# Writing the result of attention plus soft mixture of experts as whole rows instead of half rows

## The chip, the cores and the metric

The kernel runs on one core of one Trainium2 chip. The metric is the device time of one execution in microseconds (us). The kernel before takes 460.35 us (median of three runs, 460.24 to 461.63).

## The reference

```python
attn = softmax(0.125 * q @ k.T, causal) @ v          # 8 batches, 12 heads, 448 tokens, head size 64
x = attn, heads side by side                         # 3584 tokens x 768
logits = x @ phi                                     # 3584 x 32 slots
slot_in = softmax(logits, over tokens).T @ x         # 32 x 768, four slots for each of 8 experts
slot_out[e] = relu(slot_in[e] @ w1[e]) @ w2[e]       # w1 768x1024, w2 1024x768
out = softmax(logits, over slots) @ slot_out         # 3584 x 768, float32
```

All of it is float32. The two weight arrays hold 50.3 MB, the result 11.01 MB.

## The kernel before, in words

The first part, some 355 us long, is attention: 96 heads, one after another, with the order of the work on each engine written out by hand (the tuple ORDER). Of its engines only the clock and the queues matter here. While it runs, SyncE (SP) already loads the first 22 weight tiles.

The second part is the experts. Weight tiles of 128 partitions x 1536 floats (768 KB, one contiguous run of 6 KB in each partition) come through SP's queue into 34 buffers. `expert_in(e)` multiplies the slots by w1, `expert_out(e, hf)` by one half of w2's columns, where hf is 0 for columns 0 to 383 of the result and 1 for columns 384 to 767. The loads are ordered so that all tiles for hf = 0 come first, and the 16 tiles for hf = 1 last.

When `expert_out` has gone through all experts with hf = 0, `slots(0)` brings their sum into the form that the last matmul needs. It is a chain over three engines: VectorE copies the sum `so` out of PSUM, TensorE spreads it with a matmul into `rp`, ScalarE copies `rp` rounded into `sr`, and VectorE subtracts to leave the rounding rest in partitions 64 to 127 of `sr`. Then `combine(t, 0, ...)` runs for fourteen tiles t of 256 tokens, two after each `expert_out(e, 1)`. Each makes two matmuls of 128 tokens (u = 0 and 1, tile `pp`); ScalarE takes the first out of PSUM and VectorE the second, into `ot`; then SP issues one DMA of 384 KB that writes 256 pieces of 1536 bytes, half a row of the result each. After the last `expert_out` come `slots(1)` and fourteen `combine(t, 1, ...)` in the same way. So 28 DMAs write the result, and all of them stand in SP's queue behind all the weight loads. Eight DMAs of this queue are in flight at most: each has a completion semaphore out of a set that is reused in turn, and SP waits until the one it takes is free.

Every engine runs its instructions in the order in which the program issues them (`_InOrder`). `warm(n, w)` puts n matmuls on TensorE whose results nobody reads.

Of the kernel before, what the change touches and what calls it, by code (L numbers as in the profile page):

```python
# [9 lines left out]
F32 = mybir.dt.float32  # L10
F32R = mybir.dt.float32r
BF16 = mybir.dt.bfloat16
AF = mybir.ActivationFunctionType
ALU = mybir.AluOpType
# [3 lines left out]
P = 128  # L18
# [4 lines left out]
NT = NB * S  # L23
# [8 lines left out]
NR, XB = 2, 3  # L32
RES, TW1 = 22, 12
WN, PAD = 1536, 24
WARM = (3, 3, 6, 3)
START = (6, 7, 4)

# [40 lines left out]
def attention_soft_moe(ctx: ExitStack, tc: tile.TileContext, qk, va, phi, w1, w2, out):  # L80
    nc = _Core(tc)
# [28 lines left out]
    st = {}  # L110
# [11 lines left out]
    def loads_v(p, eng=nc.sync):  # L122
        if p < NPAIR:
# [4 lines left out]
    order = ([(m, e, h, u) for e in range(NEXP) for m, hs in ((0, (0, 1)), (1, (0,))) for h in hs for u in range(2)]  # L128
             + [(1, e, 1, u) for e in range(NEXP) for u in range(2)])
    NBUF = RES + TW1  # L130

    def slot(n, name, dtype=F32):
        m = n % NBUF
        pool, tag = (wres, "w") if m < RES else (wt[0], f"wa{m}")
        return pool.tile([P, WN], dtype, tag=tag, name=name)
# [40 lines left out]
    def misc(name):  # L176
        return ps_1.tile([P, 512], F32, tag="m", name=name)

    def warm(n, w=None):

        w = misc("warm") if w is None else w
        for _ in range(n):
            nc.tensor.matmul(w, identb, tri.unsqueeze(1).to_broadcast([P, w.shape[1] // P, P]),
                             start=True, stop=True)
# [53 lines left out]
    def scores1_all(i):  # L238
        for part in ("c0", "k3", "c3", "c12", "k2", "k1", "k0"):
            scores1(i, part)  # L240

    def max_evac(i):
        if i < NHD:
            st["mx", i] = (xtp.tile([P, 512], F32, tag="xt", name="mx1", bufs=2)[:, 0:S] if i == 1
                           else mx_)
            nc.scalar.activation(out=st["mx", i], in_=st["s", i][:, SC0:SC0 + S], func=AF.Copy)
# [97 lines left out]
    def logits_a(b, js, g, first=True, last=True):  # L344

        for j in js:
            xt = st.pop(("xt", b * PPB + j))
            for c in range(NCH):
                nc.tensor.matmul(g[32 * c:32 * c + 32], phis[j // 3][:, j % 3], xt[:, P * c:P * c + P],
                                 start=first and j == js[0], stop=last and j == js[-1], skip_group_check=True)  # L350
# [5 lines left out]
    def logits_b(b, l):  # L356
        bm = st["bm", b] = moe.tile([P, 1], F32, tag="bm", name=f"bm{b}", bufs=2)
        nc.vector.tensor_reduce(out=bm, in_=l, axis=AX.X, op=ALU.max, negate=True)

        mo, mn = run_m[(b + 1) % 2], run_m[b % 2]  # L360
        nc.vector.tensor_tensor(out=mn, in0=mo, in1=st.pop(("bm", b)), op=ALU.min)
# [46 lines left out]
    for b in range(NB):  # L408
        o, last = 12 * b, b == NB - 1
# [11 lines left out]

    warm(START[0])
    h0, h1 = slice(0, 1), slice(1, 2)
# [6 lines left out]
    scores1_all(1)  # L430
    warm(START[1])
    max_evac(0)
# [11 lines left out]
    scores1_all(2)  # L444
    warm(START[2])
    max_evac(2)
# [9 lines left out]
    srep = const.tile([P, 4, NSLOT], F32, name="srep")  # L456
# [23 lines left out]
    for i in range(NHD + 1):  # L480
        p, h = divmod(i, 2)
# [60 lines left out]
    b = NB - 1  # L542
# [4 lines left out]
    nc.tensor.matmul(lp, ident, lt, start=True, stop=False, skip_group_check=True)  # L547
    warm(WARM[0], wm)
    x = st.pop(("x", NPAIR - 1))
# [5 lines left out]
    logits_a(b, (4,), lp, first=False, last=False)  # L555
    warm(WARM[1], wm)
    for c in range(NCH):
        nc.tensor.matmul(lp[32 * c:32 * c + 32], phis[1][:, 2], xa[:, P * c:P * c + P],
                         start=False, stop=True, skip_group_check=True)
    logits_b(b, lp)  # L560
    warm(WARM[2], wm)

# [8 lines left out]
    for c in range(NCH):  # L571
        nc.tensor.matmul(tm[32 * c:32 * c + 32, P:P + 1], nm[:, 0:NSLOT], ident[:, 0:1],
                         start=True, stop=True, skip_group_check=True)
    warm(WARM[3], wm)
    wc, rz, sidw = (const.tile([P, n], F32, name=m) for m, n in (("wc", 1), ("rz", 1), ("sidw", NSLOT)))
# [10 lines left out]
    for hf in range(2):  # L586
        tps = (po0 if hf == 0 else po).rearrange("p a b->p (a b)")[:, 0:3 * NSLOT]
        for c in range(3):
            o = 384 * hf + P * c
            nc.tensor.matmul(tps[:, NSLOT * c:NSLOT * c + NSLOT], si[:, o:o + P], sidw,  # L590
                             start=True, stop=True)
# [23 lines left out]
    pt2 = pst.enter_context(tc.tile_pool(name="pt2", bufs=2, space=PSUM, reuse_waits="tile"))  # L615
    pso = pst.enter_context(tc.tile_pool(name="pso", bufs=4, space=PSUM, reuse_waits="tile"))
# [57 lines left out]
    so = [pt1.tile([P, 384], F32, name=f"so{i}") for i in range(2)]  # L674
    sr = const.tile([P, DM], F32R, tag="si", name="sr")
# [5 lines left out]
    def expert_out(e, hf):  # L681
        for u in range(2):
            w = wtiles[1, e, hf, u].rearrange("p (f n)->p f n", n=384)
            for g in range(4):
                fc = 4 * u + g
                nc.tensor.matmul(so[hf][32 * g:32 * g + 32], hts[e][:, fc], w[:, g],
                                 start=e == 0 and u == 0, stop=e == NEXP - 1 and u == 1,
                                 skip_group_check=True)

    def slots(hf):  # L690
        sl = slice(384 * hf, 384 * hf + 384)

        sos = c4s[-1][:, 1024:1408].bitcast(F32)
        nc.vector.tensor_copy(out=sos, in_=so[hf])
        rp = pt2.tile([P, 512], F32, tag="h", name=f"rp{hf}")
        nc.tensor.matmul(rp[:, 0:384], srep.rearrange("p a b->p (a b)"), sos, start=True, stop=True)
        nc.scalar.activation(out=sr[:, sl], in_=rp[:, 0:384], func=AF.Copy)
        nc.vector.tensor_tensor(out=sr[64:P, sl], in0=rp[64:P, 0:384], in1=sr[64:P, sl], op=ALU.subtract)

    ov = out.rearrange("(t u p) (a n) -> t p u a n", u=2, p=P, a=2)  # L700
    ntile = NT // (2 * P)

    def combine(t, hf, nb):

        if t % 2 == 0:
            st["ot"] = slot(nb, f"ot{t}_{hf}").rearrange("p (u n) -> p u n", n=384)
        ot = st["ot"][:, 2 * (t % 2):2 * (t % 2) + 2]
        for u in range(2):
            pp = pso.tile([P, 512], F32, tag="o", name=f"pp{t}_{u}_{hf}")
            o = P * (2 * t + u)  # L710
            nc.tensor.matmul(pp[:, 0:384], ct[o // WN][:, o % WN:o % WN + P],
                             sr[:, 384 * hf:384 * hf + 384], start=True, stop=True)
            if u == 0:
                nc.scalar.activation(out=ot[:, u], in_=pp[:, 0:384], func=AF.Copy)
            else:
                nc.vector.tensor_copy(out=ot[:, u], in_=pp[:, 0:384])
        nc.sync.dma_start(out=ov[t, :, :, hf], in_=ot)

    ct, c4s = [], []
    n = NBUF  # L720

    def loads(k):
        nonlocal n
        for _ in range(k):
            load_w(n)
            n += 1
# [19 lines left out]
                combine_t(b)  # L746
    expert_out(NEXP - 1, 0)
    loads(2)
    slots(0)
    for e in range(NEXP):  # L750
        expert_out(e, 1)
        for t in range(2 * e, min(ntile, 2 * e + 2)):
            combine(t, 0, len(order) + 7 + t // 2)
    slots(1)
    for t in range(ntile):
        combine(t, 1, len(order) + 7 + ntile // 2 + t // 2)
    pst.close()


# [41 lines left out]
```

## Time and the profile before

| | us |
|---|---|
| median of three runs | 460.35 |
| time of the profiled execution | 459.88 |
| its span, first to last instruction | 458.2 |
| last weight tile landed | 429.31 |
| `slots(1)` starts, first matmul of `combine(0, 1)` | 430.27, 433.25 |
| last instruction of a compute engine ends | 443.7 |

Times in the profile count from the span's start. PE is TensorE's matmuls, PEld its weight loads, DVE VectorE, ACT ScalarE, SPq the sequencer of SyncE, which issues the DMAs. A row of the windows view holds the stretch, its length, the busy time of PE, PEld, DVE, ACT and POOL with their counts of instructions, then the granted TensorE clock as a share of full speed, the busy share of the sixteen DMA engines (over 1 where packets overlap) and the rate in GB/s. In a timeline row stand start, length, engine and instruction. In a row of DMA issues stand the size of one and the median us from issue to landing.

### The profile page before, as it was taken

To read this page: it belongs to the slowest core of one execution; us is meant where nothing else is said; L and a number is where in the kernel's file an instruction comes from. 1 tells how busy PE (TensorE), PEld (TensorE's weight loads), DVE (VectorE), ACT (ScalarE), POOL (GpSimd) and SP (SyncE) were. 2 spreads that over 40 slices of the span, in tenths; PEclk is the share of its full clock that TensorE was granted. 3 is DMA by queue.
4 is the path that set the end of the run, shared out by engine and by line. 5 is a ranking of instruction groups with operands and counts; after the bars stand their busy time and mean duration, and the time that the engine had idled before them with its cause. 6 is when DMAs were issued, how large, how long until landed. Compare 5 with 4: busy or idle time off the path is not lost.

```text
span 458.2 us, 12014 instructions
## 1 busy us (share of the span) xinstructions
PE 424.9 (93%) x4581; PEld 362.3 (79%) x4581; DVE 348.9 (76%) x1044; ACT 329.9 (72%) x496; POOL 266.3 (58%) x215
## 2 busy tenths in 40 slices
PE   6899999999999999999999999999999998996660
PEld 3798999999899989998999999999989654542230
DVE  6988888888888898888888888888886467332350
ACT  6898899889888988897899789988975211342240
POOL 5888777777777777777778777777771000000000
PEclk9999999999999999999999999999999999999875
DMA  7477666676667765777666766667758999999997
GB/s 267 128 259 243 235 193 224 216 239 223 204 208 237 236 221 171 241 241 231 210 188 225 254 222 216 191 213 253 231 160 300 369 411 415 414 414 413 402 391 284
DMA packets 38201, 119.04 MB, mean 260 GB/s; under 512 B 4096, under 2 KB 11776, under 8 KB 38144
## 3 DMA queue, kind: packets, MB, share of 16 engines
q1 hardware_dynamic: 38000, 118.01, 75.6%
q8 instruction: 36, 0.59, 0.5%
q10 hardware_dynamic: 144, 0.27, 0.2%
q14 instruction: 21, 0.17, 0.1%
HBM read 107.25 MB, written 11.01 MB: 258 GB/s over the span
## 4 chain that ended last, share of the span: by engine, by line
PE 77%; DMA 11%; POOL 5%; ACT 1%; DVE 1%; issue 1%; SPq 0%; POOLq 0%; ACTq 0%
PE po L64 34%; PE s L64 24%; DMA w<-in_w_dram 10%; PE xt L64 4%; PE g L64 3%; PE hp L64 3%; POOL r L64 3%; PE sp L64 2%; PE rt L64 2%; PE pp L64 2%; POOL ks L64 1%; PE e L64 1%; PE so L64 1%; DMA qk<-in_qk_dram 1%; ACT ot L64 0%
## 5 line engine op out<-in xcount | busy, mean ns | idle before, releaser
L64 PE MATMUL po<-va,pt 128*128 128x65 f32 x1900 | 193.6, 250 | 0.1
L64 PEld LDWEIGHTS po<-va,pt 128*128 128x128 f32 x1900 | 190.5, 171 | 0.5 <-issue 0.3
L64 DVE TENSOR_TENSOR mx<-s,mx 128x320 f32<-128x320 f32 (+2 forms) x288 | 100.8, 350 | 31.4 <-ACT mx L64 27.9
L64 POOL TENSOR_TENSOR r<-qk,qd 64x896 fp32r<-64x896 f32 (+1 forms) x50 | 101.5, 2030 | 6.5 <-ACT qd L64 2.7
L64 POOL TENSOR_SCALAR_AFFINE_SELECT r<-mr 14x448 fp32r<-14x448 f32 x96 | 61.4, 640 | 73.2 <-DVE mr L64 72.8
L64 ACT ACTIVATE pt<-s 128x1024 f32<-128x1024 f32 x96 | 98.2, 1023 | 6.3 <-PE s L64 3.1
L64 POOL TENSOR_TENSOR ks<-qk,ks 64x896 fp32r<-64x896 f32 (+1 forms) x47 | 98.1, 2087 | 4.5 <-ACT ks L64 0.9
L64 PE MATMUL s<-r,k 128*128 128x320 f32 (+3 forms) x384 | 83.2, 298 | 2.3 <-POOL r L64 2.2
L64 ACT ACTIVATE mx<-s 128x448 f32<-128x448 f32 x96 | 52.5, 546 | 36.0 <-PE s L64 22.2
L64 PE MATMUL s<-qd,ks 128*128 128x448 f32 (+3 forms) x384 | 76.0, 308 | 1.6 <-ACT qd L64 1.6
L64 PEld LDWEIGHTS s<-r,k 128*128 128x128 f32 (+1 forms) x384 | 60.0, 176 | 6.4 <-POOL r L64 2.9
L64 DVE STREAM_TRANSPOSE mt<-mx 128x448 f32<-128x448 f32 x96 | 61.9, 645 | 3.3
L64 DVE TENSOR_REDUCE r<-mt 128x14 f32<-128x448 f32 x96 | 58.4, 609 | 0.1
L64 PEld LDWEIGHTS s<-qd,ks 128*128 128x128 f32 (+1 forms) x384 | 55.0, 180 | 3.1 <-ACT qd L64 2.3
L64 ACT ACTIVATE ks<-qk 128x896 fp32r<-128x896 f32 (+1 forms) x50 | 45.6, 914 | 2.5 <-DMA qk<-in_qk_dram 2.5
L64 ACT ACTIVATE k<-ks 64x896 fp32r<-64x896 f32 (+1 forms) x49 | 45.8, 935 | 1.1
L64 ACT ACTIVATE qd<-qk 128x896 fp32r<-128x896 f32 (+1 forms) x50 | 46.1, 923 | 0.4 <-DMA qk<-in_qk_dram 0.3
L64 PEld LDWEIGHTS <-identb 128*128 128x128 bf16 x320 | 28.1, 99 | 20.1 <-issue 15.8
L64 DVE TENSOR_TENSOR x<-po,sm 128x256 f32<-128x256 f32 x95 | 40.3, 424 | 3.3
L64 PE MATMUL s<-tri,identb 128*128 128x64 bf16 (+2 forms) x288 | 39.7, 234 | 0.2
L64 ACT ACTIVATE xts<-xt 128x512 f32<-128x512 f32 x47 | 28.1, 598 | 6.7 <-PE xt L64 4.4
L64 PE MATMUL so<-w,ht 128*32 128x384 f32 x256 | 24.9, 492 | 7.4 <-DMA w<-in_w_dram 5.6
(124 smaller groups left out, 396.2 us busy)
## 6 DMA issues: line engine op xcount, KB each, us to landing
w<-in_w_dram SPq DMA_DIRECT2D x64, 768.0 KB, 7.5
qk<-in_qk_dram SPq DMA_DIRECT2D x94, 448.0 KB, 3.5
va<-in_va_dram SPq DMA_DIRECT2D x47, 260.0 KB, 3.5
out_dram<-ot SPq DMA_DIRECT2D x28, 384.0 KB, 6.5
qk<-in_qk_dram SPq DMA_DIRECT2D x4, 224.0 KB, 3.3
va<-in_va_dram ACTq DMA_DIRECT2D x1, 260.0 KB, 5.4
phi<-in_phi_dram SPq DMA_DIRECT2D x2, 48.0 KB, 3.9
```

Source lines behind the costliest of these rows:

```text
L64: return self._tc.keep_in_program_order(op(*args, **kwargs))
```

## The change

1. The DRAM rows are dealt out otherwise: partition p of tile t holds tokens 256t + 2p and 256t + 2p + 1, which lie next to each other in DRAM. The matmul takes every second column of `ct` for it.
2. `ot` of a tile is one buffer for both halves of the columns (two tokens x 768 floats in a partition). For tiles 6 to 13 the first half is only kept, and after the second half one DMA writes the tile: 768 KB, 128 pieces of 6144 bytes. Tiles 0 to 5 (FILL = 6) are written as before, in two DMAs of 384 KB. There are 20 DMAs instead of 28.
3. With hf = 1, tiles 6 to 13 are combined first and tiles 0 to 5 last.
4. `slots(1)` runs its chain twice, for 192 columns each; four idle matmuls stand ahead of the first `rp`, and four behind the second.

```diff
-WARM = (3, 3, 6, 3)
+WARM = (3, 3, 6, 3, 4, 4)
+FILL = 6
...
-    def slots(hf):
...
+    def slots(hf, parts):
+        for a, z in parts:
+            sl = slice(384 * hf + a, 384 * hf + z)
+
+            sos = c4s[-1][:, 1024 + a:1024 + z].bitcast(F32)
+            nc.vector.tensor_copy(out=sos, in_=so[hf][:, a:z])
+            if hf and a == 0:
+                warm(WARM[4], pso.tile([P, 512], F32, tag="o", name="warm1")[:, 0:384])
+            rp = pt2.tile([P, 512], F32, tag="h", name=f"rp{hf}_{a}")[:, 0:z - a]
+            nc.tensor.matmul(rp, srep.rearrange("p a b->p (a b)"), sos, start=True, stop=True)
+            nc.scalar.activation(out=sr[:, sl], in_=rp, func=AF.Copy)
+            nc.vector.tensor_tensor(out=sr[64:P, sl], in0=rp[64:P], in1=sr[64:P, sl], op=ALU.subtract)
+        if hf:
+            warm(WARM[5], pso.tile([P, 512], F32, tag="o", name="warm2")[:, 0:384])
+
-    ov = out.rearrange("(t u p) (a n) -> t p u a n", u=2, p=P, a=2)
+    ov = out.rearrange("(t p u) n -> t p u n", u=2, p=P)
...
+    def combine(t, hf):
+        if hf == 0:
+
+            ots[t] = slot(len(order) + 7 + t, f"ot{t}").rearrange("p (u n) -> p u n", u=2)
+        ot, sl, o = ots[t], slice(384 * hf, 384 * hf + 384), 2 * P * t
         for u in range(2):
             pp = pso.tile([P, 512], F32, tag="o", name=f"pp{t}_{u}_{hf}")
-            o = P * (2 * t + u)
-            nc.tensor.matmul(pp[:, 0:384], ct[o // WN][:, o % WN:o % WN + P],
-                             sr[:, 384 * hf:384 * hf + 384], start=True, stop=True)
+            nc.tensor.matmul(pp[:, 0:384], ct[o // WN][:, o % WN + u:o % WN + 2 * P:2],
+                             sr[:, sl], start=True, stop=True)
...
-        nc.sync.dma_start(out=ov[t, :, :, hf], in_=ot)
+        if t < FILL:
+            nc.sync.dma_start(out=ov[t, :, :, sl], in_=ot[:, :, sl])
+        elif hf:
+            nc.sync.dma_start(out=ov[t], in_=ot)
...
-    slots(0)
+    slots(0, ((0, 384),))
...
-    slots(1)
-    for t in range(ntile):
-        combine(t, 1, len(order) + 7 + ntile // 2 + t // 2)
+    slots(1, ((0, 192), (192, 384)))
+    for t in [*range(FILL, ntile), *range(FILL)]:
+        combine(t, 1)
```

## Rows read from the trace of the kernel before

**Rows 1.** The page, the span in 40 slices: rate of the DMA engines.

```profile
GB/s 267 128 259 243 235 193 224 216 239 223 204 208 237 236 221 171 241 241 231 210 188 225 254 222 216 191 213 253 231 160 300 369 411 415 414 414 413 402 391 284
```

**Rows 2.** Windows view: weight stream, output stream and its parts, and the clock's fall.

```profile
400.00:424.00 24.00, 19.32 (x158) 8.50 (x162) 6.99 (x14) 7.64 (x18) 0.00 (x0) 1.00 1.02 414
...
428.00:457.00 29.00, 11.30 (x43) 6.23 (x38) 8.63 (x17) 6.92 (x15) 0.00 (x0) 0.68 0.99 366
430.00:440.00 10.00, 7.89 (x25) 4.70 (x21) 5.48 (x11) 4.64 (x10) 0.00 (x0) 0.66 1.06 399
444.00:456.00 12.00, 0.00 (x0) 0.00 (x0) 0.00 (x0) 0.00 (x0) 0.00 (x0) 0.54 0.96 352
456.00:457.00 1.00, 0.00 (x0) 0.00 (x0) 0.00 (x0) 0.00 (x0) 0.00 (x0) 0.50 0.13 46
...
430.00:432.00 2.00, 1.32 (x6) 0.30 (x2) 0.56 (x1) 0.00 (x0) 0.00 (x0) 0.85 1.06 399
```

**Rows 3.** Chain that ended last, from the last weight load to `combine(0, 1)`.

```profile
413.94 15.37 DMA w<-in_w_dram
...
430.27 0.57 DVE c L64
...
430.89 1.20 PE rp L64 x2
...
432.63 0.57 DVE sr L64
...
433.25 5.13 PE pp L64 x13
```

**Rows 4.** Timeline of SyncE's queue: loads and writes, one issue a row.

```profile
370.67 0.39 SPq L64 DMA_DIRECT2D w<-in_w_dram  x1
371.21 0.34 SPq L64 DMA_DIRECT2D w<-in_w_dram  x1
...
415.84 0.41 SPq L64 DMA_DIRECT2D out_dram<-ot  x1
...
442.52 1.14 SPq L64 DMA_DIRECT2D out_dram<-ot  x1
443.75 1.13 SPq L64 DMA_DIRECT2D out_dram<-ot  x1
```

**Rows 5.** DMA issues of 400 to 415, 428 to 440 and 451 to 458 us.

```profile
w<-in_w_dram SPq DMA_DIRECT2D x8, 768.0 KB, 15.4
...
out_dram<-ot SPq DMA_DIRECT2D x10, 384.0 KB, 7.5
...
out_dram<-ot SPq DMA_DIRECT2D x3, 384.0 KB, 4.1
```

**Rows 6.** Timeline: `slots(0)`, `combine(8, 0)` at full clock, `combine(0, 1)` at half.

```profile
403.99 0.91 PE L64 MATMUL rp<-c,srep 128*128 128x384 f32 x2 [0.68 <-DVE c L64]
...
418.49 0.97 PE L64 MATMUL pp<-sr,ct 128*128 128x384 f32 x4
...
419.14 1.02 DVE L64 COPY ot<-pp 128x384 f32<-128x384 f32 x2 [2.76 <-PE pp L64]
...
434.29 1.90 DVE L64 COPY ot<-pp 128x384 f32<-128x384 f32 x3 [1.10 <-DMA out_dram<-ot]
```

**Rows 7.** Groups by form, 350 to 445 us, and timeline of `warm`: smaller pieces.

```profile
L64 DVE COPY xta<-e 128x256 f32<-128x256 f32 x1 | 0.4, 425 | 0.8 <-PE e L64 0.8
...
L64 ACT ACTIVATE ct<-cp 128x192 fp32r<-128x192 f32 x1 | 0.3, 328 | 0.0
...
360.50 0.83 PE L64 MATMUL po<-tri,identb 128*128 128x256 bf16 x6
...
362.16 0.50 PE L64 MATMUL po<-tri,identb 128*128 128x256 bf16 x3
```

**Rows 8.** Span's start: SyncE's first issue, and DMA rate in slices of 0.1 us.

```profile
0.81 2.77 SPq L64 DMA_DIRECT2D qk<-in_qk_dram  x6
...
GB/s 0 0 0 0 0 0 0 0 0 0 0 0 0 0 0 0 0 0 90 54 90 143 125 251 340 340 412 412 287 287 358 430 394 394 269 161 143 125 125 90
```

More of the change, by code (lines that the diff above doesn't have):

```diff
@@ L688, in expert_out @@
                                  skip_group_check=True)
-    def slots(hf):
[L691 to L698, printed above, removed]
@@ L700, in attention_soft_moe @@
-    ov = out.rearrange("(t u p) (a n) -> t p u a n", u=2, p=P, a=2)
[L701 to L707, printed above, removed]
+    def slots(hf, parts):
[11 more added lines that the diff above has]
+            warm(WARM[5], pso.tile([P, 512], F32, tag="o", name="warm2")[:, 0:384])
@@ L708, in combine @@
+    ov = out.rearrange("(t p u) n -> t p u n", u=2, p=P)
+    ntile, ots = NT // (2 * P), {}
+    def combine(t, hf):
+        if hf == 0:
+            ots[t] = slot(len(order) + 7 + t, f"ot{t}").rearrange("p (u n) -> p u n", u=2)
+        ot, sl, o = ots[t], slice(384 * hf, 384 * hf + 384), 2 * P * t
         for u in range(2):
             pp = pso.tile([P, 512], F32, tag="o", name=f"pp{t}_{u}_{hf}")
-            o = P * (2 * t + u)
-            nc.tensor.matmul(pp[:, 0:384], ct[o // WN][:, o % WN:o % WN + P],
-                             sr[:, 384 * hf:384 * hf + 384], start=True, stop=True)
+            nc.tensor.matmul(pp[:, 0:384], ct[o // WN][:, o % WN + u:o % WN + 2 * P:2],
+                             sr[:, sl], start=True, stop=True)
@@ L713, in combine @@
             if u == 0:
-                nc.scalar.activation(out=ot[:, u], in_=pp[:, 0:384], func=AF.Copy)
+                nc.scalar.activation(out=ot[:, u, sl], in_=pp[:, 0:384], func=AF.Copy)
             else:
-                nc.vector.tensor_copy(out=ot[:, u], in_=pp[:, 0:384])
-        nc.sync.dma_start(out=ov[t, :, :, hf], in_=ot)
+                nc.vector.tensor_copy(out=ot[:, u, sl], in_=pp[:, 0:384])
+        if t < FILL:
+            nc.sync.dma_start(out=ov[t, :, :, sl], in_=ot[:, :, sl])
+        elif hf:
+            nc.sync.dma_start(out=ov[t], in_=ot)
@@ L752, in attention_soft_moe @@
         for t in range(2 * e, min(ntile, 2 * e + 2)):
-            combine(t, 0, len(order) + 7 + t // 2)
-    slots(1)
-    for t in range(ntile):
-        combine(t, 1, len(order) + 7 + ntile // 2 + t // 2)
+            combine(t, 0)
+    slots(1, ((0, 192), (192, 384)))
+    for t in [*range(FILL, ntile), *range(FILL)]:
+        combine(t, 1)
     pst.close()
```

## The prediction

> **What bounds the kernel now.** I read the page's 40 slices first. The rate of the DMA engines lies between 128 and 300 GB/s as long as attention runs and at 391 to 415 from slice 33 on, to fall to 284 in the last [rows 1]. The change touches only this last part, so I cut it into stretches. From 400 to 424 us the weights stream at 414 GB/s with the DMA engines busy for 1.02 of the time [rows 2]. From 430 to 440 the result is written at 399 with a share of 1.06. From 444 to 456 no compute engine does anything, yet the rate is only 352 with a share of 0.96. The chain of waits says the same from the other side: it hangs on the last weight load (413.94 + 15.37 = 429.31), goes through `slots(1)` to the matmuls of `combine` at 433.25 [rows 3], and leaves the compute engines 14 us ahead of the span's end. What sets the end is bytes through the DMA engines. The last bytes move at about 457.0.
>
> Why 352 and not 399? SP's queue answers. Two writes in a row are 443.75 - 442.52 = 1.23 us apart, each 1.13 us of issuing; two weight loads of twice the size with half as many pieces are 0.54 apart, and a write with nothing right ahead of it takes 0.41 [rows 4]. At 1.23 us a write of 393,216 bytes gives 320 GB/s, less than the engines can take. While there is a backlog this is hidden; the time from issue to landing shows it being eaten up, 7.5 us at 428 to 440 and 4.1 at the end [rows 5]. So the last 12 us are bound by issuing, which costs 12 x (1 - 352/399) = 1.4 us. That is all the issuing can give back.
>
> **The change part by part.**
>
> *Larger writes.* 28 x 393,216 = 11.01 MB are written in both. From 428 on 29 x 366 = 10.61 MB move, so 0.40 MB of the result had gone before. Eight tiles (6.29 MB) now go in pieces of 6144 bytes. No row shows such a write. The nearest rows are reads in the same pieces (414) and writes in pieces a quarter as long (399) [rows 2]; they are the bounds. I take 414, since the piece's length is what the DMA engine sees in both: 6.29/0.399 = 15.8 us become 6.29/0.414 = 15.2, a gain of 0.6. With the lower bound it is 0.
>
> The Trainium skill, page "DMA: Bandwidth & Descriptors", section Specifications, puts the smallest transfer for line rate at 512 B; by it pieces of 1536 B are as good as 6144 and the 0.6 is not there. The 399 beside 414 speaks mildly against it, but writes and reads are not the same thing.
>
> *Fewer issues.* Eight issues of some 0.5 us replace sixteen of 1.2. Whole tiles bring 768 KB each, 1.9 us of DMA work, so the backlog grows, and the six half writes at the end come behind it: the 1.4 us come back, unless the low rate at the end has another reason than issuing (then 0).
>
> *What fills the DMA engines while slots(1) runs.* This speaks against the change. Before, fourteen writes stand ready, and the engines have work until far past 433. Now only six do. Their matmuls are done long before, so they go in behind the weights at unchanged times. At 428, 2.36 - 0.40 = 1.96 MB of them are left; at 398 they are out at 428 + 4.9 = 432.9. What comes next is tile 6 as a whole, and it needs `slots(1)` and both evictions.
>
> When is that? `so` ends at 430.25 as before, 0.02 ahead of the copy [rows 3]. The chain now runs twice for 192 columns, and VectorE takes its instructions in order: the second copy stands behind the first subtract, which waits for ScalarE, which waits for TensorE. The two halves don't overlap. A VectorE copy takes 0.57 for 384 columns [rows 3] and 0.42 for 256 [rows 7], so 0.35 for 192; ScalarE takes 0.33 [rows 7]. `rp` takes 0.91 for 384 columns at full clock [rows 6]; half of it is 0.46, all of it 0.91, and 0.58 is my value (streaming halves, the pipeline's depth does not). The four idle matmuls ahead: six of 256 columns take 0.83 and three 0.50 [rows 7], 0.11 each, so 0.165 for 384 columns and 0.66 for four. They end at 430.91, 0.25 after the first copy (430.27 + 0.35 + 0.04). Then `rp` to 431.49, ScalarE to 431.84, subtract to 432.21, second copy to 432.58, `rp` from 432.62 to 433.20, ScalarE to 433.55, subtract to 433.92. The second four idle matmuls end at about 433.7 and hide behind these. First `pp`: 433.96 instead of 433.25. At full clock VectorE starts its eviction 0.65 after the first `pp` [rows 6] and needs 0.56: 435.2. From SP's first issue to the first bytes at the span's start 1.0 us pass (0.81 to 1.8) [rows 8]. So new bytes move at 436.2. The gap is 436.2 - 432.9 = 3.3 us, with no work in the queue to cover it. Bounds: 2.3, if the halves did overlap or were one; 4.3 with TensorE at half clock (below).
>
> *Order, strides, buffers.* Later tiles are no bottleneck: three evictions in a row take VectorE 1.90 us [rows 6], so a tile comes every 0.6 against 1.9 us of DMA work. A stationary operand taken from every second column may load slower; no row shows it, and between nothing and a doubling of some 0.2 us it lies beside that 1.9. The kept tiles need buffers earlier, but these held weights used up long before. Eight DMAs in flight are enough: eight whole tiles are 15 us of work. All taken as 0.
>
> *The sum.* From 428 to 456, when all but 0.05 MB is out [rows 2], the kernel before spends 28 us. The changed one: to 436.2, then 15.2 us of whole tiles and 2.36/0.399 = 5.9 of half ones: 457.3. Before, a trickle of 46 GB/s follows for 1 us [rows 2], one lagging engine by its rate; a gap lets laggards catch up, so I take half of it, 0.5 (bounds 0 and 1). The last bytes move at 457.8 instead of 457.0: +0.8 us. In terms: gap +3.3, issuing -1.4, piece length -0.6, trickle -0.5. The profiled execution took 459.88, 1.7 more than its span for what lies around it, and would take 460.7. The median of the runs is 0.47 above it, so 461.2 against 460.35.
>
> **The rivals.**
>
> *The gap is covered (faster).* The slowest DMA engine is late: the last weights land at 429.31, though at 428 almost all are there. If the lag is spread over many engines, their six halves last to 429.3 + 5.9 = 435.2, and new bytes at 435.2 (halves overlapping, or the chain shorter than my sum) meet them. Then only the gains stay: -1.4 - 0.6 = -2.0, 458.4. It decides once tile 6 is in SP's queue by about 434. For it: the 1.3 us of lag. Against it: the chain's bound of 2.3 us after 432.9.
>
> *The clock falls all the same (slower).* Before, 430 to 432 shows a mean of 0.85 and 430 to 440 one of 0.66 [rows 2]: TensorE went from 2.4 to 1.2 GHz at about 431.4 (0.3 of 2 us lost, at half speed), after it had idled for most of each wait for weights and for 0.6 us ahead of `rp`. The first four idle matmuls fill that last hole, hence my full clock. If it falls nevertheless, the second `rp` takes 0.3 longer, the second four take 1.3 instead of 0.66 and push the first `pp` to 434.6, and VectorE starts 1.04 after it, as at 433.25 and 434.29 [rows 3, 6], not 0.65. New bytes move at 437.2: +1.0 on the sum, +1.8, 462.2.
>
> *The end's rate is not SP's (slower).* Writing may slow down late for a reason in memory, with any issue. Then 1.4 us don't come back: +2.2, 462.6. The Trainium skill's same page, section "Issuing engines are not separate DMA queues", calls the issuing time usually small against the transfer, which speaks for it; here it is 1.13 us against 0.98 of transfer at 399, which does not agree [rows 4].
>
> *One engine sets everything (no change).* If one DMA engine alone is late by 1.3 us throughout, before ends at 429.3 + 11.01/0.399 = 456.9 without any loss to issuing. The issuing gains nothing, but the gap costs that engine 1.0 only: 436.2 + 15.2 + 5.9 = 457.3, +0.4, 460.8.
>
> **How the numbers follow.** My forecast has 0.43, covered gap 0.15, clock 0.20, end's rate 0.12, one engine 0.10. A measurement of this kernel tells about 0.3% (1.4 us: 459.0 to 461.7) from no change. Forecast and one engine lie inside, 0.53; the covered gap is faster, 0.15; the other two slower, 0.32. The forecast's own range is 460.0 to 462.0 (piece length, trickle, `rp`); its edge past 461.7 is about as likely as a clock rival that stays below. The range for all, 458.8 to 462.6, holds a gap covered in part and leaves out the fully covered one and the upper half of the end's rate.
>
> **What would show it.** Right: a hole of 2 to 4 us in the DMA rate between 433 and 437, first `pp` of tile 6 at about 434, clock at 1.00 through 431 to 438, 410 GB/s or more while whole tiles go out, and 399 for the last six halves. Wrong: no hole, or one that starts after 434 (the first rival); the clock at 0.5 in `slots(1)` (the second); 350 GB/s in the last 6 us with a backlog (the third). The sum fails most easily in the 1.0 us from issue to first bytes, taken from the span's start, and in 6144-byte writes, which no row shows.

## The result, and the profile after

The changed kernel takes 462.61 us (median of 22 runs) against 460.88 of 22 runs of the kernel before in the same rounds. The ratio is 1.0033, with a 95% interval of 1.0020 to 1.0047: 0.9 to 2.2 us slower. The forecast was 461.2 against 460.35 (a ratio of 1.0018), the range 458.8 to 462.6; on the forecast's base of 460.35 the measured ratio gives 461.9.

The page of the changed kernel shows the difference at once. Before, its DMA slices stay at 391 GB/s or more from slice 33 until the last one, at 284 [rows 1]; now the third from the end has 289:

```profile
GB/s 233 142 274 233 221 193 225 235 234 218 194 214 244 233 218 177 236 239 234 211 187 227 246 229 216 192 210 256 228 143 312 384 396 414 414 414 415 289 413 338
```

The windows view of the changed kernel, against [rows 2]: the weight stream as before, then a hole, whole tiles, and the six half tiles at the end (columns as ahead: the last three are clock, DMA share and GB/s).

```profile
400.00:424.00 24.00, 19.11 (x164) 8.12 (x158) 7.16 (x14) 6.77 (x16) 0.00 (x0) 1.00 1.02 415
...
432.00:438.00 6.00, 4.43 (x24) 2.60 (x21) 2.89 (x7) 2.21 (x6) 0.00 (x0) 1.00 0.50 187
439.00:444.00 5.00, 4.24 (x17) 2.59 (x17) 4.25 (x9) 3.78 (x10) 0.00 (x0) 1.00 1.02 412
...
453.60:459.60 6.00, 0.00 (x0) 0.00 (x0) 0.00 (x0) 0.00 (x0) 0.00 (x0) 0.50 1.04 370
```

From 432 to 438 the engines move 187 GB/s instead of 399: 6 x (1 - 187/399) = 3.2 us' worth of transfer is lost, taken over all sixteen engines (their common rate). The chain of waits of the changed kernel tells why the hole is so long; it answers to [rows 3]:

```profile
416.17 15.06 DMA w<-in_w_dram
...
432.13 0.76 PE warm L66 x4
432.88 0.34 PE rp L66 x2
...
433.61 0.36 DVE sr L66
...
433.98 0.37 DVE c L66
...
434.40 0.61 PE rp L66 x2
...
435.39 0.37 DVE sr L66
...
435.80 0.46 PE pp L66
```

The second copy (`c`, 433.98) starts when the first subtract (`sr`, 433.61) is over: the two halves stand in a row. The last weights landed at 416.17 + 15.06 = 431.23, the first `pp` runs 4.57 later; before it was 433.25 - 429.31 = 3.94.

SP's queue in the changed kernel, one issue a row, answers to [rows 4]: the sixth write, the first whole tile 9.6 us behind it, and two whole tiles while data move.

```profile
427.53 1.01 SPq L66 DMA_DIRECT2D out_dram<-ot  x1
...
437.09 0.36 SPq L66 DMA_DIRECT2D out_dram<-ot  x1
...
440.31 1.16 SPq L66 DMA_DIRECT2D out_dram<-ot  x1
441.57 1.19 SPq L66 DMA_DIRECT2D out_dram<-ot  x1
```

Since the moment at which the last weights land differs from profile to profile (below), ends are compared from there. Before: 458.2 - 429.3 = 28.9 us to the span's end. After: 461.0 - 431.2 = 29.7. That is 0.8 us for the end of the kernel, 0.2%.

### The profile page after: what moved, and what is told of

The parts are those of the page before. It is cut to its first block, busy times and chain, and to the rows that moved or that the text cites. A ratio compares the mean times of both kernels' runs of the same rounds, so it can differ in the third digit from the quotient of the medians.

```text
span 461.0 us, 12020 instructions
## 1 busy us (share of the span) xinstructions
PE 427.2 (93%) x4591; PEld 363.2 (79%) x4591; DVE 349.2 (76%) x1046; ACT 330.0 (72%) x497; POOL 266.5 (58%) x215
## 4 chain that ended last, share of the span: by engine, by line
PE 74%; DMA 11%; POOL 5%; DVE 3%; ACT 2%; issue 1%; SPq 0%; POOLq 0%; ACTq 0%
PE po L66 34%; PE s L66 24%; DMA w<-in_w_dram 10%; PE xt L66 4%; PE g L66 3%; POOL r L66 3%; PE sp L66 2%; PE rt L66 2%; POOL ks L66 1%; PE e L66 1%; DMA qk<-in_qk_dram 1%; DVE lm L66 1%; PE pp L66 1%; DVE lg L66 1%; ACT ot L66 1%
## 5 line engine op out<-in xcount | busy, mean ns | idle before, releaser
L66 DVE TENSOR_TENSOR mx<-s,mx 128x320 f32<-128x320 f32 (+2 forms) x288 | 100.9, 350 | 32.2 <-ACT mx L66 28.5
L66 PE MATMUL s<-qd,ks 128*128 128x448 f32 (+3 forms) x384 | 77.2, 312 | 2.1 <-ACT qd L66 2.1
L66 PEld LDWEIGHTS <-identb 128*128 128x128 bf16 x328 | 29.1, 101 | 21.6 <-issue 17.3
```

What stands on the lines that cost most here:

```text
L66: return self._tc.keep_in_program_order(op(*args, **kwargs))
```

## The experiments

All were timed in five rounds beside the kernel before, except the two second profiles, which are one run each. "End" is the time from the landing of the last weights to the span's end, in one profile of each kernel; the second profiles came within 0.1 us of the first. The expectations count to the last byte, some 1.2 us less.

| kernel | ratio to before (95%) | end, us |
|---|---|---|
| before; second profile | 1 | 28.9; 28.8 |
| changed; second profile | 1.0033 (1.0020 to 1.0047) | 29.7; 29.7 |
| held_back | 1.0054 (1.0031 to 1.0077) | 31.4 |
| no_warm | 1.0040 (1.0017 to 1.0063) | 30.1 |
| whole_last | 1.0030 (1.0011 to 1.0050) | 30.0 |
| unsplit | 1.0024 (1.0001 to 1.0048) | 28.8 |
| fill14 | 0.9997 (0.9977 to 1.0018) | 28.6 |
| two_queues | 0.9995 (0.9971 to 1.0019) | 29.1 |
| split_only | 0.9993 (0.9968 to 1.0018) | 28.9 |
| fill8_unsplit | 0.9990 (0.9969 to 1.0012) | 27.8 |
| fill10_unsplit | 0.9984 (0.9963 to 1.0005) | 28.1 |
| fill10 | 0.9974 (0.9951 to 0.9996) | 28.1 |

### fill10: more work for the gap

```diff
-FILL = 6
+FILL = 10
```

> The changed kernel with FILL = 10 instead of 6: ten tiles written in halves, four whole. In the changed kernel the DMA engines run dry between 432.8 and 437.9 us, worth 3.2 us of transfer. Theory (the loss is this gap): four more half tiles are 1.57 MB, 3.9 us of work, ahead of the first whole tile, so the gap is all but gone. After it come 4 whole tiles (7.6 us at 412 GB/s) and 10 halves (10.6 us at the 371 seen at the end of the changed kernel): the last bytes 24.9 us after the last weight tile lands, if the DMA engines are in step, instead of 28.5; total about 459.0 against 462.6. Rival (the slowest DMA engine sets the end): its six halves already lasted until 436.5, so the gap costs it only 1.4 us, and more halves at 371 cost 0.5: about 27.6 after the weights, total about 461.7. Rival (the gap costs nothing, the second split chain or the layout does): no change, 28.5 and 462.6.

Measured: 460.08 us, ratio 0.9974, faster than the kernel before by 0.26% with an interval that just leaves out 1, and faster than the changed kernel. The windows view of fill10:

```profile
432.00:438.00 6.00, 4.43 (x20) 2.62 (x19) 3.07 (x7) 2.68 (x7) 0.00 (x0) 1.00 1.06 399
439.00:444.00 5.00, 3.95 (x15) 2.11 (x14) 4.26 (x9) 3.62 (x8) 0.00 (x0) 1.00 1.03 426
448.00:452.00 4.00, 0.00 (x0) 0.00 (x0) 0.00 (x0) 0.00 (x0) 0.00 (x0) 0.50 1.06 394
452.00:456.00 4.00, 0.00 (x0) 0.00 (x0) 0.00 (x0) 0.00 (x0) 0.00 (x0) 0.50 0.99 369
```

The same stretch 432 to 438 runs at 399, so the gap was the loss. The end is 1.6 us shorter than in the changed kernel, between the 3.6 that engines in step would have given and the 0.9 of the slowest engine; how much of the gap the slowest engine feels is worked out in the section on the prediction. And two rates differ that should not: whole tiles go at 426 here and at 412 in the changed kernel, half tiles at 394 for a while against 370.

### unsplit: the chain in one piece

```diff
-    slots(1, ((0, 192), (192, 384)))
+    slots(1, ((0, 384),))
```

> The changed kernel with slots(1) run once over 384 columns, both groups of idle matmuls kept. Theory (the two halves of the chain follow one another on VectorE, so that the split only lengthens it): copy 0.57, rp 0.91, ScalarE 0.5, subtract 0.57 and some 0.1 between them, 2.65 us instead of 3.68 from the end of so to the first pp with the clock at full: the first whole tile is issued 1.0 us earlier, the gap is 1.0 shorter, total 461.6 against 462.6. Rival (the halves overlap somewhere or the slowest DMA engine sets the end): 0 to 0.3 us.

Measured: ratio 1.0024, end 28.8 instead of 29.7, as the theory had it. The timeline of unsplit has the first `pp` at 435.42, 3.66 after its last weights (431.76) instead of 4.57:

```profile
432.72 0.56 DVE L66 COPY c<-so 128x384 f32<-128x384 f32 x1 [2.23 <-PE so L66]
433.33 0.91 PE L66 MATMUL rp<-c,srep 128*128 128x384 f32 x2
...
434.81 0.56 DVE L66 TENSOR_TENSOR sr<-rp,sr 64x384 fp32r<-64x384 f32 x1 [1.53 <-ACT sr L66]
435.42 0.81 PE L66 MATMUL pp<-sr,ct 128*128 128x384 f32 x3 [0.53 <-DVE sr L66]
```

The time is 0.8 us less than the changed kernel's by the medians and 0.4 by the ratios, and the intervals overlap; the 0.9 of the end does not hang on them.

### split_only: the same chain where there is no gap

```diff
 (in the kernel before)
-    slots(0)
+    slots(0, ((0, 384),))
...
-    slots(1)
+    slots(1, ((0, 192), (192, 384)))
```

with the changed kernel's `slots` and its eight idle matmuls.

> The kernel before with the split chain and the eight idle matmuls of the change alone; 28 half writes, all fourteen of the first half ready. Theory (a longer chain costs time only where the DMA engines run dry meanwhile): first pp some 4.5 us after the last so instead of 3.9, no hole in the DMA rate, 27.6 us from the last weights to the last byte, total 461.1 as before (within 0.3%). Rival (the chain costs its own length wherever it stands): 0.6 to 0.9 more, 461.9.

Measured: 0.9993, end 28.9. The longer chain costs nothing behind fourteen ready writes. So the 0.9 us that it costs in the changed kernel is the gap's.

### no_warm: the clock

```diff
-WARM = (3, 3, 6, 3, 4, 4)
+WARM = (3, 3, 6, 3, 0, 0)
```

> The changed kernel without the eight idle matmuls in slots(1). Theory (they keep TensorE at full clock): the clock falls to half while slots(1) runs, as in the kernel before, the second rp takes 0.3 longer, pp to eviction 0.4 longer, but the first rp starts 0.1 to 0.2 earlier: first whole tile 0.5 us later, total 463.1. Rival (the clock stays at full anyway): first whole tile 0.1 to 0.2 earlier, total 462.5.

Measured: 1.0040, end 30.1, 0.4 more than the changed kernel. The windows view of no_warm has the clock at half where the changed kernel has 1.00:

```profile
433.00:440.00 7.00, 6.19 (x18) 4.14 (x17) 4.05 (x8) 3.79 (x9) 0.00 (x0) 0.52 0.56 228
```

The first whole tile is issued 0.4 us later than in the changed kernel, counted from the last weights (6.23 and 5.86 us); 0.5 was expected. The difference in time (0.07%) is too small for the interval. That the idle matmuls alone hold TensorE at 2.4 GHz is more than the runs show. In all nine profiles with them the clock is at 1.00 through `slots(1)`, but without them it fell in three (before, held_back, no_warm) and stayed at 1.00 in two (two_queues and the second profile of the kernel before), with the same waits ahead of it. The windows view of that second profile, where [rows 2] has 0.66:

```profile
430.00:440.00 10.00, 6.69 (x30) 3.44 (x30) 5.50 (x11) 4.63 (x11) 0.00 (x0) 1.00 1.06 398
```

So without them the fall comes in some executions only. In the kernel before it costs nothing that the end shows: 28.9 us with the fall, 28.8 without.

### held_back: the gap alone

```diff
 (in the kernel before)
+        if hf == 0 and t >= 6:
+            held.append((t, ot))
+            return
         nc.sync.dma_start(out=ov[t, :, :, hf], in_=ot)
+        if hf and held:
+            t0, ot0 = held.pop(0)
+            nc.sync.dma_start(out=ov[t0, :, :, 0], in_=ot0)
...
-    ct, c4s = [], []
+    ct, c4s, held = [], [], []
```

> The kernel before, with one thing of the change alone: the writes of tiles 6 to 13 of the first half are held back, and one goes out behind each of the first eight writes of the second half. All 28 writes stay halves of 384 KB. Times from the last weight tile's landing to the last byte: 27.6 us in the kernel before, 28.5 in the changed one. The first new bytes come some 6.3 after the weights; 22 half tiles are 8.65 MB. Theory A (a gap costs its own length and no more, halves go at the 399 GB/s seen before): 6.3 + 21.7 = 28.0, total 0.4 above before, 461.3. Theory B (a gap also brings all 16 DMA engines into step, and engines in step write halves at 371, as at the end of the changed kernel): 6.3 + 23.3 = 29.6, total 2.0 above before, 462.9. Against the changed kernel, the same gap with whole rows, B says that whole rows save some 1.1 us, A that they save nothing.

Measured: 463.49 us, 1.0054, end 31.4, 2.5 more than before; theory B had 2.0 and A 0.4. The windows view of held_back:

```profile
432.00:436.00 4.00, 2.82 (x9) 2.18 (x9) 2.06 (x4) 2.02 (x5) 0.00 (x0) 0.50 0.40 149
436.00:458.00 22.00, 6.86 (x21) 3.75 (x21) 6.23 (x12) 5.34 (x11) 0.00 (x0) 0.66 1.01 364
```

After the gap the half tiles go at 364 GB/s from the first microsecond, at a time at which the kernel before still writes the same pieces at 399 [rows 2]. A gap thus cost more than its length here. Whether that is the engines or SP, this run alone does not tell: from 436.5 on SP's issues come 1.08 us apart on average, which for 384 KB is 364 GB/s as well. whole_last, below, does tell. The whole rows take part of the loss back: the changed kernel has the gap too, and its end is 1.7 us shorter; 6.29 MB take 17.3 us at 364 and 15.3 at 412.

### whole_last: the order turned round

```diff
-    for t in [*range(FILL, ntile), *range(FILL)]:
+    for t in range(ntile):
```

> The changed kernel with the order of the second half turned round: the six half tiles first, the eight whole tiles last. Theory (SP's issuing bounds half tiles when no backlog stands ahead of them, 1.2 us for 384 KB): the six halves after the gap take 7.4 us instead of 6.4, at 320 GB/s, then the whole tiles 15.3 at 412: total 1.0 us above the changed kernel, 463.6. Rival (half tiles are slow late in the kernel for a reason in memory, not for SP): the halves take what they took, and the whole tiles at the end go at 385 instead of 412, 1.0 us more; the rate of the last 8 us tells the two apart (412 or 385). Rival (writes of the second half of the columns are slow wherever they stand): halves at 371 GB/s directly after the gap, the same total.

Measured: 1.0030, end 30.0, only 0.3 above the changed kernel. The windows view of whole_last, half tiles and then whole ones:

```profile
440.00:444.00 4.00, 3.44 (x14) 2.17 (x14) 3.45 (x7) 3.11 (x8) 0.00 (x0) 1.00 1.01 367
446.00:460.00 14.00, 0.00 (x0) 0.00 (x0) 0.00 (x0) 0.00 (x0) 0.00 (x0) 0.52 1.02 414
```

The halves are not slowed to 320 GB/s by issuing: that theory misses. SP issues the six within 4.0 us (438.09 to 442.13), faster than the 1.07 us apart at which they land, so issuing does not set the 367. Nor are writes slow because they come late: whole tiles go at 414 to the end. Halves after a gap go at 367 to 370 whether they stand ahead of the whole tiles or behind them. That writes of the second half of the columns are slow as such was the third guess; fill10 speaks against it, with such writes at 394.

### two_queues: is it SP?

```diff
 (in the kernel before)
-        nc.sync.dma_start(out=ov[t, :, :, hf], in_=ot)
+        (nc.scalar if hf and t % 2 else nc.sync).dma_start(out=ov[t, :, :, hf], in_=ot)
```

> The kernel before, with every second write of the second half issued by ScalarE instead of SP. Theory (in the last 12 us SP's issuing, 1.22 us for 384 KB, keeps the DMA engines at 352 GB/s): two queues issue fast enough, the rate stays at 399 to the end, 1.4 us less, total 459.5; if the engines in step can do 371 at best, 0.6 us less, 460.3. Rival (the low rate has its cause behind the DMA engines): no change, 460.9, with a rate near 350 and time from issue to landing of 8 us or more instead of 4 to 5.

Measured: 0.9995, no change, as the rival had it. The windows view of two_queues, and its DMA issues of 446 to 454 us:

```profile
430.00:440.00 10.00, 6.18 (x25) 2.88 (x25) 4.67 (x9) 3.11 (x7) 0.00 (x0) 1.00 1.06 399
446.00:454.00 8.00, 1.79 (x4) 0.79 (x3) 1.48 (x3) 0.98 (x2) 0.00 (x0) 0.50 1.04 367
```

```profile
out_dram<-ot SPq DMA_DIRECT2D x4, 384.0 KB, 8.9
out_dram<-ot ACTq DMA_DIRECT2D x2, 384.0 KB, 7.0
```

Now 7 to 9 us pass from issue to landing, so work is waiting, and the rate falls to 367 all the same. SP is no limit here: from 440 on its issues come 1.3 to 2.2 us apart, and each takes some 0.4 us while data move, as this row of SP's timeline in two_queues shows:

```profile
440.26 0.37 SPq L64 DMA_DIRECT2D out_dram<-ot  x1
```

The Trainium skill, page "DMA: Bandwidth & Descriptors", section "Issuing engines are not separate DMA queues", says that issuing from several engines saves only the issuing time, since all run on the same 16 DMA engines; this run agrees (ratio 0.9995).

### fill14, fill10_unsplit, fill8_unsplit: the parts that are left, and a better version

```diff
-FILL = 6
+FILL = 14
```

> The changed kernel with FILL = 14: the new order of the rows and the split chain stay, but every tile is written in halves, fourteen ahead of the second half. Theory (the gap and the larger pieces are all that matters; the two tokens in a partition and the longer chain cost nothing once the DMA engines have work): no gap, 28 halves as before: 27.6 us after the weights, total 460.9. Rival (the chain or the strided operand costs time of its own): 0.5 to 1 above that. Rival (issuing limits the end of the kernel before, and the order of the rows changes nothing on that): the last 12 us at some 350 GB/s again, the same total as the theory.

Measured: 0.9997, end 28.6. The new order of the rows and the operand of every second column cost nothing that the ratio or the end shows; without whole tiles nothing is gained either.

```diff
-FILL = 6
+FILL = 10
-    slots(1, ((0, 192), (192, 384)))
+    slots(1, ((0, 384),))
```

> The changed kernel with FILL = 10 and slots(1) run once over 384 columns. FILL = 10 alone gave 26.6 us after the weights and 0.26% less than the kernel before; the unsplit chain alone shortened the time to the first whole tile by 0.9 us. Theory (with ten fillers part of the DMA engines still ran dry for up to 1 us): 0.3 to 0.6 less than with FILL = 10 alone, 26.1 to 26.3 after the weights, total 459.6. Rival (the slowest DMA engine had no gap left): no change against FILL = 10 alone, 460.1.

Measured: 0.9984, end 28.1 as in fill10: the rival was right, with ten fillers there is no gap left to shorten. Its whole tiles go at 423, from 439 to 446.

The third has FILL = 8 in the same place.

> The changed kernel with FILL = 8 and the chain unsplit: with 10 fillers the last byte came 26.6 us after the last weights. Theory (whole rows go at 430 GB/s against 399 for halves as long as the DMA engines are not in step, and eight fillers just cover the 5.7 us from the last weights to the first whole tile for all engines but the most advanced): 0.3 less than with ten, 26.3, total 459.9. Rival (with eight some engines run dry, a part of them comes into step): 0.3 to 0.6 more than with ten, 27.0, total 460.7.

Measured: 0.9990, end 27.8, the shortest of all by 0.3, which is less than the times can tell. Its DMA rates in slices of 0.15 us have a short dip, to 143 GB/s, and after it whole tiles go at 413: some of each theory. Of the three versions that keep eight or ten writes ready (fill10, fill10_unsplit, fill8_unsplit), fill10 is the one whose interval leaves out 1.

### A second profile of each

> The kernel before, unchanged, once more, for a second profile. If the 27.6 us from the last weights to the last byte are a property of the kernel they come out within 0.3 again, and the rate falls from 399 to some 350 GB/s in the last 12 us again; when the last weights land may differ by 1 to 3 us, with the clock granted in the first 25 us.

> The changed kernel, unchanged, for a second profile. If its end is a property of the kernel, span's end comes 29.7 us after the last weights again (28.9 and 28.8 in two profiles of the kernel before), with a hole of some 4 us in the DMA rate and the whole tiles at 412 GB/s. When the last weights land (431.2 in the first profile, 429.3 and 430.6 before) hangs on the clock of the first 15 us: if that is chance, it may come anywhere from 429.3 to 432.5; if it belongs to the changed kernel, above 431.

The ends came out as in the first profiles (28.8, 29.7). The last weights landed at 430.6 in the second profile of the kernel before and at 428.2, the earliest of all, in the second of the changed one. So the 431.2 of the first profile is no property of the changed kernel. In that profile the clock was low for a while at the start, as the windows view of the changed kernel's PE shows:

```profile
5.00:15.00 10.00, 7.69 (x37) 0.83 0.85 285
```

## Why the prediction came out as it did

**The bound, right.** Bytes through the DMA engines set the end, and what the change does to the time it does there; the weight stream is the same (414 and 415 GB/s).

**The gap, right in kind, and in size for the common rate.** Forecast were 3.3 us without work and new bytes 6.9 us after the last weights. The DMA rate of the changed kernel from 432 to 440, in slices of 0.2 us:

```profile
GB/s 415 392 407 402 399 376 361 323 300 269 261 215 200 169 154 154 131 123 100 92 46 54 38 8 0 0 0 0 0 215 430 338 492 461 399 399 369 338 492 461
```

The rate sinks from 433.0 on and is zero at 436.8; new bytes move at 437.8, 6.6 us after the weights. The 3.2 us lost and the chain's terms agree with the sum: first `pp` 4.57 after the weights (forecast 4.65), first issue 1.29 after it (1.24), bytes 0.7 after the issue (1.0). unsplit shortened the gap, no_warm lengthened it, fill10 took it away, and the end followed; split_only has the longer chain without a gap, and its end stayed. What the gap costs the end is less than 3.2 us, though (below).

**Larger writes, right in size.** Forecast were 414 GB/s for whole tiles; they go at 409 to 414 after a gap and 423 to 426 without one. That the figure, read from weight loads, met the first of the two is in part luck: the forecast had no reason for the difference.

**Fewer issues, wrong.** This is the step of the prediction that failed: that issuing holds the last 12 us of the kernel before at 352 GB/s, and that 1.4 us of its end come back. SP's 1.2 us an issue are real, but in the changed kernel a whole tile with half as many pieces takes 1.16 to 1.19 too when one issue follows another, against 0.36 for the first. So the number of pieces does not set that time; what does, no run shows. two_queues took the limit away, and its end is no shorter (29.1 us). The rival "the end's rate is not SP's" was nearer: with a deep backlog the six half tiles at the end of the changed kernel go at 370, not at the 399 of the sum, and cost 6.4 us instead of 5.9. From 454 to 458, when SP has issued all, the rate is 370 still. What that rival had wrong is that whole tiles don't suffer.

**The trickle, mis-sized.** Half a microsecond was put down for it. The changed kernel has hardly any; its rate from 456 to 460, in slices of 0.1 us, ends within 0.2:

```profile
GB/s 399 369 384 353 384 354 384 338 384 384 369 384 369 353 369 354 384 338 399 369 384 384 353 384 353 384 338 384 353 384 353 415 323 399 369 338 123 0 0 0
```

In the kernel before, the rate sank from 307 at 455.8 to 15 at 456.9. In the changed kernel by itself the halves' 0.5 too little and the trickle's 0.4 too much nearly cancel, so the 28.5 us that the sum has from the last weights to the last byte came out.

**What the sum left out: the engine that ends last.** The sum counts the sixteen DMA engines as one pipe with one rate. The trace has sixteen landings for each DMA, one for each engine's part (without the engine's name), and in every run the span ends 0.8 to 1.1 us after the very last of them. In the kernel before, the last parts of the 28 writes land 0.94 to 1.09 us apart, from the weights at 429.31 to 457.33: the last engine always has work, and SP costs it nothing. The first parts land up to 3.5 us earlier. It is the engines that are ahead which wait for SP: from 444 to 454 the first parts come 1.16 to 1.26 us apart, SP's pace, and the lead shrinks to 1.1 us. That lowers the common rate, and it explains why nothing comes back when the issuing is taken away.

In the changed kernel the last part of the sixth half write lands at 437.05 and that of the first whole tile at 440.42. The DMA issues of the changed kernel at 427.53 and 437.09 have it, from issue to landing:

```profile
out_dram<-ot SPq DMA_DIRECT2D x1, 384.0 KB, 9.5
...
out_dram<-ot SPq DMA_DIRECT2D x1, 768.0 KB, 3.3
```

A whole tile takes 1.9 us of these 3.37, so the engine that ends last is without work for 1.5 us, not for 3.3. The other runs bear that out; all times are from one last landing to another:

| kernel | last half write ahead of the whole tiles to first whole tile, us | last weights to last write, us |
|---|---|---|
| before | no whole tiles | 28.0 |
| changed; second profile | 3.37; 3.37 | 28.9; 28.9 |
| no_warm | 3.75 | 29.2 |
| unsplit | 2.46 | 28.0 |
| fill10 | 1.84 | 27.0 |
| fill8_unsplit | 1.85 | 26.8 |

Counted by that engine, against 28 half writes at 1.0 us, the changed kernel has +1.5 for the gap, -0.8 for eight whole tiles at 1.9 instead of sixteen halves, and +0.2 for the other halves (0.97 us each ahead of the gap, 1.06 behind it): +0.9 us. The forecast had +3.3 for the gap, -1.4 and -0.5 for issuing and trickle, -0.6 for the length of the pieces. So, as causes, its gap was 1.8 too large and what issuing and trickle give back was 1.9 too large; the two cancel. That the total agrees with the +0.8 of the ends rests on something else: the sum took the stretches of the changed kernel one by one (first new bytes, whole tiles, halves), which hold for every engine once all start together behind the gap, and compared them with the measured end of the kernel before. The rival "one engine sets everything", which had a chance of 0.10, had this mechanism; its +0.4 is too low, because it had the gap at 1.0 and the last halves at 399 GB/s.

**The clock, right; its reason only in part.** It stayed at 1.00 through `slots(1)` (432 to 438). The prediction took the fall in the one profile of the kernel before for a property of that kernel; the second profile, without the fall, shows that it is not.

**The time.** The interval of the ratio starts at 0.9 us, just above the 0.8 that the ends show, and its middle is 1.5. In the chances, "no change" had 0.53 and "slower" 0.32; at 0.33% the measured time lies at the border of the two, on the slower side. Where the other 0.7 us would be, if it is not chance, no run shows: in the profiles the last weights land between 429.3 and 430.6 us for the kernel before and its variants (five), and between 428.2 and 432.5 for the changed kernel and its variants (nine), with no work different until the first half's `combine`. In one of the five and in five of the nine (one of them the profile above) the clock is at half for 3 to 7 us somewhere between 8 and 25 us. Nothing that the change touches has run by then, which speaks for chance, but the timed runs without a profile have no such rows. That stays open.

## What to carry to other kernels

Where transfers set the end, look at what is in their queue while a chain of dependent work runs, before looking at the size of the pieces: larger writes that become ready later trade queued work for efficiency, and here 1.5 us without work, for the engine that ends last, stood against 0.8 us of better writes. Ask which of the engines ends last, and whether it waits: the common rate can fall, as in the last 12 us of the kernel before, because the engines that are ahead wait, and that costs nothing. Keep as many small writes back in the queue as the chain is long (here ten tiles instead of six turned 0.33% slower into 0.26% faster). A queue's issue time read from a trace says little by itself about who limits whom; issue the same work from a second queue and see.

## What the hardware showed that was not expected

After a gap in the DMA work the 16 engines go in step, and then they write more slowly. The landings show the first part: the sixteen parts of the last write ahead of the gap land over 3.4 us in the changed kernel, those of each write behind it within 0.25 us, until the end. For the second part stand the rates of the same pieces: half tiles 399 GB/s without a gap ahead (before, 430 to 440; fill10, 394) and 364 to 370 after one (held_back, whole_last, the changed kernel); whole tiles 423 to 426 without and 409 to 414 after. For the last engine that is 0.98 us against 1.06 a half tile and 1.85 against 1.90 a whole one. That being in step is the cause is argued, not shown. The kernel before speaks for it: with no gap ahead, its last parts go from 0.98 to between 1.02 and 1.09 us apart at about 448, just when more than half of the engines have come to land within 0.2 us of the first; only the last write is faster again. two_queues speaks against it: its rate falls to 367 although the first and the last part of each write land 1.9 us and more apart, and for that no run tells why.

Writes in pieces of 1536 bytes are slower than writes in pieces of 6144, by 6% without a gap (399 and 423 to 426) and by 11% after one (370 and 412). The two also differ in the size of one DMA (384 and 768 KB), and no run separates that from the piece. The Trainium skill, page "DMA: Bandwidth & Descriptors", section Specifications, puts the smallest transfer for line rate at 512 B; if it is the piece that counts, the runs here differ from that, and they decide.
